# Value products of one attention tile and scores of the next in one run with shared banks; low half of the gated product at the head of a step

## The chip, the core and the metric

The kernel runs on one core of a Trainium2 chip. Its engines work side by side, each through its own instructions in order, and wait for each other by semaphores: TensorE (PE in the rows; PEld is its weight load), VectorE (DVE), ScalarE (ACT), GpSimd (POOL), and SyncE (SP), which here issues all transfers. The metric is the device time of one execution in microseconds, the median of the runs.

## The reference, cut to what matters

```python
# attention in chunks of 64 tokens, 8 heads of 64
scores = scale * np.matmul(q_c, k_c.transpose(0, 1, 2, 4, 3))
attn = np.exp(scores - np.max(scores, axis=-1, keepdims=True))
attn = attn / (np.sum(attn, axis=-1, keepdims=True) + 1e-09)
out = np.matmul(attn, v_c)
# then x of 4608 tokens x 512 through a gated layer of 512 x 1536 x 512,
g = x @ w_gate
silu = g * (1.0 / (1.0 + np.exp(-g)))
val = x @ w_val
y = silu * val @ w_out
# then x / rms * rms_g, and a second gated layer of the same form
```

## The kernel before, in words

The program is written in the order in which each engine runs it: no scheduler moves anything. The first layer works on 9 blocks of 512 tokens, and a block in 12 steps of 128 hidden features (the loop at L1024). Every matrix is held as a high and a low part, so each product is three matmuls of 128x512 (`mm3`, L441).

A step has three groups of 12 matmuls on TensorE: g (`emit_g`), v (`emit_v`) and y (`emit_y`). The y of a step is that of the step before (`prev`). On ScalarE a tanh follows g (L454); on VectorE `product` (L455) makes the gate of it, `v_product` (L471) multiplies by v, ScalarE casts the result to its high part hh (L474), and `lo` (L476) subtracts to give the low part hl. hh and hl feed the y of the next step, where hl is needed by the second matmul (L443). g and v have one PSUM bank each, y has four, and the two banks a0 and a1 are left for attention and for the sums of squares.

Attention comes in 36 tiles of 128 tokens, those of a block during the block before it. From tile 8 on a tile is: `trans_att` (VectorE transposes q and k, L305), `att_s` (32 small matmuls, scores into a0 and a1), `att_m` (VectorE maxima and subtractions L341, L342, ScalarE exp), `att_n` (sums and reciprocal, then GpSimd multiplies), `att_td` in two halves (VectorE transposes p, L376), `att_pv` (32 small matmuls into new tiles in a0 and a1, then two ScalarE copies to xh, L427), and `att_lo` (VectorE, low part xl, L436).

What is done where is set by a table: `put` hangs a function on a position, three positions to a step. Position 0 of a step runs after g, 1 after v and `product`, 2 after y and `v_product` (L1053 to L1069). Before, the tiles of a block start at positions 0, 8, 16 and 24 of its 36. Also in the table: the sums of squares of the block before (`rms_*`; their two matmuls, ssq, use a0), the loads of q, k and v by SP, and, every second step, the loading and conversion (L115 to L121) of a second-layer weight, of which GpSimd, ScalarE and SP make combinations. Step 0 of a block ends the y of the block before, which `evac_y` copies out of PSUM. In block 0 VectorE also converts the weights of the first layer (`conv1`).

The second layer (L1089 on) follows on the same core and has no part in the change.

Of the kernel before, what the change touches and what calls it, by code (L numbers as in the profile page):

```python
# [9 lines left out]
F32 = mybir.dt.float32  # L10
# [9 lines left out]
def tile_kernel(  # L20
# [19 lines left out]
    NT, DM = out.shape  # L40
    DFF = moe_w_gate.shape[1]
    P = 128
    CH = 64
# [267 lines left out]

    prob = {}

    def att_s(i, tags=("a0", "a1")):
        qT, kT = qkT.pop(i)
        sb = [ps.tile([P, 512], F32, tag=tags[z], name=f"s{z}_{i}") for z in range(2)]
        for hp in range(HP):
            for x in range(2):
                for hpar in range(2):
                    c = hpar ^ x  # L320
                    nc.tensor.matmul(
                        sb[x][c * 64:c * 64 + 64, hp * 64:hp * 64 + 64],
                        qT[hp][hpar * 64:hpar * 64 + 64, c * 64:c * 64 + 64],
                        kT[hp][hpar * 64:hpar * 64 + 64, c * 64:c * 64 + 64],
                        start=True,
                        stop=True,
                    )
        score[i] = sb
# [75 lines left out]

    xps = {}

    def att_pv(i, j, tags=("a0", "a1")):
        pT = probT.pop(i)
        xb = [ps.tile([P, 512], F32, tag=tags[c], name=f"xb{c}_{i}") for c in range(2)]
        xb = [t[:, :HP * CH].rearrange("p (h c) -> p h c", h=HP) for t in xb]  # L410
        for hp in range(HP):
            for c in range(2):
                g, n = where[2 * i + c]
                vt = gt[g][2]
                for hpar in range(2):
                    z = (hpar ^ c) * 64
                    nc.tensor.matmul(
                        xb[c][hpar * 64:hpar * 64 + 64, hp, :],
                        vt[z:z + 64, hp, n, :],
                        pT[z:z + 64, hp, c * 64:c * 64 + 64],  # L420
                        start=True,
                        stop=True,
                    )
        xh, xl = x_tiles(0, j)
        o = i * P - blocks[j][0]
        for c in range(2):
            nc.scalar.copy(xh[:, :, o + c * CH:o + (c + 1) * CH], xb[c])  # L427
        xps[i] = xb

    def att_lo(i, j):  # L430
        xb = xps.pop(i)
# [159 lines left out]
    def spread(l, j, pos, n, make):  # L591
# [7 lines left out]
        for z in range(n):  # L599
            put(l, j, pos + z, lambda z=z: step(z))  # L600

    for x, (l, j) in enumerate(seq):
        if x + 1 < len(seq):
            nl, nj = seq[x + 1]
            if nl == 0:
                for n, i in enumerate(tiles_of(nj)):
                    b = 8 * n if x else (0, 11, 19, 26)[n]
                    if i >= 8:
                        put(l, j, b - 1, lambda i=i: trans_att(i))
                    else:  # L610
                        put(l, j, b, lambda i=i: trans_tok(i, ("a0", "a1")))
                    e = 1 if i < 8 else 0
                    put(l, j, b + 1 + e, lambda i=i: att_s(i))
                    put(l, j, b + 2 + e, lambda i=i: att_m(i))
                    put(l, j, b + 3 + e, lambda i=i: att_n(i))
                    if i < 8:
                        put(l, j, b + 6, lambda i=i: att_t(i))
                    else:
                        put(l, j, b + 4, lambda i=i: att_td(i, 0))
                        put(l, j, b + 5, lambda i=i: att_td(i, 1))  # L620
                    e = 0 if i < 8 else 1
                    put(l, j, b + 8 - e, lambda i=i, nj=nj: att_pv(i, nj))
                    put(l, j, b + 9 - e, lambda i=i, nj=nj: att_lo(i, nj))
                    for c in (2 * i, 2 * i + 1):
                        g = where[c][0]
                        if g > 0 and c == groups[g][-1] and g + 2 < len(groups):
                            d = 10 if i < EARLY else 1
                            spread(l, j, b + d, 8, lambda g=g: load_qk(g + 2))
                            spread(l, j, b + d + 8, 3, lambda g=g: load_v(g + 2))
        if x > 0 and seq[x - 1][0] == 0:  # L630
            pj = seq[x - 1][1]
            for d in range(KD):
                put(l, j, 3 + 2 * d, lambda pj=pj, d=d: rms_sq(pj, d))
            put(l, j, 12, lambda pj=pj: rms_split(pj))
            put(l, j, 14, lambda pj=pj: rms_mm(pj))
            for z in range(4):
                put(l, j, 18 + 2 * z, lambda pj=pj, z=z: rms_rec(pj, z))
            put(l, j, 26, lambda pj=pj: rms_newton(pj))
            for d in range(KD):
                put(l, j, 28 + 2 * d, lambda pj=pj, d=d: rms_x(pj, d))  # L640

# [287 lines left out]
    with tc.manual_schedule():  # L929
# [94 lines left out]
        for n, (l, j, f) in enumerate(iters):  # L1024
            def run(p):
                for fn in at.get(3 * n + p, ()):
                    fn()

            head = (l, j) == (0, 0)
            if (j, f) == (1, 0):  # L1030
                conv.close()
                cv = open_pool(conv, "cv2", 2, "right")
            if (j, f) == (NB - 1, 0):
                conv.close()
                attn.close()
                X2 = open_pool(two, "x2", 1, "right")
                x_load(0, 0)
                xops = x_prep(0, 0)
            if (j, f) == (NB - 1, 8):
                x_load(0, 1)  # L1040
                xops = xops + x_prep(0, 1)
            if (j, f) == (NB - 1, 8):
                load_ring(16)

            if head and f == 0:
                issue(later + load_tok(5))
            if head and f in (1, 2):
                issue(load_tok(5 + f))
                if f == 1:
                    issue(load_v(2))  # L1050
            if n + 2 < len(iters) and n + 2 >= NF:
                load_lo(*iters[n + 2])
            sg, product = emit_g(l, j, f)  # L1053
            run(0)
            if prev is not None:
                lo()
            if head:
                conv1(3 * f + 7)
            v_product, lo = emit_v(l, j, f, sg)
            product()  # L1060
            run(1)
            if head:
                conv1(3 * f + 8)
            if prev is not None:
                emit_y(*prev)
                if prev[2] == NF - 1:
                    evac_y(*prev[:2])
            v_product()
            run(2)  # L1069
            if head:  # L1070
                conv1(3 * f + 9)
            if j == NB - 1 and f >= 2:
                for _ in range(3 if f > 6 else 2):
                    if xops:
                        xops.pop(0)()
            prev = (l, j, f)
# [109 lines left out]
```

## Time and profile before

| | us |
|---|---|
| median of three runs | 1839.19 (1836.37 to 1842.35) |
| the profiled execution, its time | 1840.34 |
| its span, first to last instruction | 1838.5 |
| TensorE busy in the span | 1781.2 (97%) |
| VectorE busy | 1275.0 (69%) |
| ScalarE busy | 661.4 (36%) |
| GpSimd busy | 389.9 (21%) |

A busy TensorE is not one at its peak: the end of a matmul is modelled and rows overlap, so a row's length tells little and the distance from one row's start to the next tells how fast it goes. Times in the rows are in us from the start of the span, and a bracket at a row's end gives the idle time of its engine before it and who ended it.

### The profile page before, as it was taken

How to read it: one execution, taken by the hardware profiler on the slowest of the kernel's cores; microseconds unless marked ns; L12 is line 12 of the kernel's file. 1: busy time of each engine (PE TensorE's matmuls, PEld its weight loads, DVE VectorE, ACT ScalarE, POOL GpSimd, SP SyncE). 2: the span in 40 equal slices, each digit the busy share in tenths (PEclk: the TensorE clock that was granted, in tenths of full speed). 3: DMA queues.
4: the chain of work that ended last, by engine and by line, in shares of the span. 5: the costliest groups of instructions: out<-in, count | busy, mean ns of one | idle time of the engine just before them, and what ended most of it. 6: DMA issues, size and time to landing. Idle time of an engine off the chain costs nothing.

```text
span 1838.5 us, 31037 instructions
## 1 busy us (share of the span) xinstructions
PE 1781.2 (97%) x11094; PEld 1518.3 (83%) x11094; DVE 1275.0 (69%) x2358; ACT 661.4 (36%) x1254; POOL 389.9 (21%) x391
## 2 busy tenths in 40 slices
PE   5989999999999999999999999999999999999999
PEld 4767787877878777787888778988898889999999
DVE  7986887877778687886735466845694477468465
ACT  4543322323233233323223333533462344335334
POOL 1001325342343433424022200200020011002000
PEclk7989999999999999999999999999999999999999
DMA  9986667776668676675344476677667767887885
GB/s 250 265 239 159 175 188 212 206 235 163 212 175 232 191 203 214 192 225 160 98 134 164 151 230 193 212 228 215 191 213 229 210 188 235 255 264 262 272 245 182
DMA packets 385034, 379.86 MB, mean 207 GB/s; under 512 B 200048, under 2 KB 235888, under 8 KB 384880
## 3 DMA queue, kind: packets, MB, share of 16 engines
q1 hardware_dynamic: 384880, 377.87, 69.1%
q8 instruction: 89, 1.46, 0.3%
q14 instruction: 65, 0.53, 0.1%
HBM read 316.41 MB, written 61.34 MB: 205 GB/s over the span
## 4 chain that ended last, share of the span: by engine, by line
PE 80%; DVE 10%; DMA 4%; SPq 2%; POOL 2%; ACT 2%; issue 1%; DVEq 0%; ACTq 0%; POOLq 0%
PE y L443 5%; PE ygA L882 4%; PE y L442 4%; PE y L444 4%; PE g L442 4%; PE v L442 4%; PE g L444 4%; PE g L443 4%; PE v L444 4%; PE v L443 4%; PE yvA L882 4%; PE ygC L882 2%; PE yvC L882 2%; DVE pT L376 2%; DVE hl L476 1%
## 5 line engine op out<-in xcount | busy, mean ns | idle before, releaser
L443 PE MATMUL y<-hl,wo 128*128 128x512 f32 x432 | 174.6, 404 | 20.6 <-DVE hl L476 20.4
L442 PE MATMUL y<-hh,wo 128*128 128x512 f32 x432 | 175.2, 406 | 0.0
L442 PE MATMUL g<-xh,wg 128*128 128x512 f32 x432 | 171.7, 397 | 1.2 <-ACT xh L427 0.9
L444 PE MATMUL y<-hh,lo 128*128 128x512 f32 x432 | 171.7, 398 | 0.0
L442 PE MATMUL v<-xh,wv 128*128 128x512 f32 x432 | 170.2, 394 | 1.3 <-DVE sg L471 1.3
L443 PE MATMUL g<-xl,wg 128*128 128x512 f32 x432 | 169.4, 392 | 1.6 <-DVE xl L436 1.6
L444 PE MATMUL g<-xh,lg 128*128 128x512 f32 x432 | 169.3, 392 | 1.0 <-DMA lg<-lo_scratch 1.0
L444 PE MATMUL v<-xh,lv 128*128 128x512 f32 x432 | 168.3, 390 | 0.0
L443 PE MATMUL v<-xl,wv 128*128 128x512 f32 x432 | 168.2, 389 | 0.0
L455 DVE SCALAR_TENSOR_TENSOR sg<-sg,g 128x512 f32<-128x512 f32 x108 | 73.8, 684 | 127.5 <-ACT sg L454 127.4
L454 ACT ACTIVATE sg<-g 128x512 f32<-128x512 f32 x108 | 64.5, 597 | 252.1 <-PE g L444 252.0
L822 POOL TENSOR_TENSOR h<-h,h 128x512 f32<-128x512 f32 (+1 forms) x30 | 37.0, 1234 | 550.9 <-DVE h L800 550.9
L376 DVE STREAM_TRANSPOSE pT<-p 32x128 f32<-32x128 f32 x448 | 135.6, 303 | 11.3 <-POOL p L360 5.2
L474 ACT CAST hh<-sg 128x512 fp32r<-128x512 f32 x108 | 67.1, 622 | 194.2 <-DVE sg L471 193.7
L858 DVE TENSOR_TENSOR hl<-h,hh 128x512 fp32r<-128x512 f32 (+1 forms) x180 | 122.4, 705 | 13.1 <-ACT hh L857 13.0
L443 PEld LDWEIGHTS y<-hl,wo 128*128 128x128 f32 x432 | 83.2, 193 | 45.8 <-DVE hl L476 29.6
L857 ACT CAST hh<-h 128x512 fp32r<-128x512 f32 (+1 forms) x180 | 98.8, 576 | 41.0 <-PE yvA L882 26.1
L783 ACT ACTIVATE sig<-sgt 128x512 f32<-128x512 f32 (+1 forms) x90 | 53.0, 589 | 155.9 <-DVE sgt L791 155.8
L360 POOL TENSOR_TENSOR p<-p,r 128x512 f32<-128x512 f32 x36 | 43.3, 1203 | 286.3 <-DVE r L359 248.8
L784 DVE TENSOR_TENSOR sgt<-sgt,sig 128x512 f32<-128x512 f32 (+1 forms) x90 | 57.7, 641 | 61.7 <-ACT sig L783 61.7
L471 DVE SCALAR_TENSOR_TENSOR sg<-v,sg 128x512 f32<-128x512 f32 x108 | 73.7, 682 | 36.3 <-PE v L444 35.1
L442 PEld LDWEIGHTS y<-hh,wo 128*128 128x128 f32 x432 | 82.9, 192 | 18.9
(769 smaller groups left out, 4619.8 us busy)
## 6 DMA issues: line engine op xcount, KB each, us to landing
wrg<-w_scratch SPq DMA_DIRECT2D x210, 256.0 KB, 3.1
wrv<-w_scratch SPq DMA_DIRECT2D x210, 256.0 KB, 3.1
wro<-w_scratch SPq DMA_DIRECT2D x210, 256.0 KB, 3.0
lg<-lo_scratch SPq DMA_DIRECT2D x96, 256.0 KB, 2.9
lv<-lo_scratch SPq DMA_DIRECT2D x96, 256.0 KB, 3.4
lo<-lo_scratch SPq DMA_DIRECT2D x96, 256.0 KB, 3.8
w_scratch<-wsg SPq DMA_DIRECT2D x42, 256.0 KB, 2.4
w_scratch<-wsv SPq DMA_DIRECT2D x42, 256.0 KB, 2.7
```

Source lines behind the costliest of these rows:

```text
L376: nc.vector.transpose(out=pT[o:o + 32, :, r:r + 32], in_=pt[r:r + 32, :, z, b * 32:b * 32 + 32])
L442: nc.tensor.matmul(o, sh, mh, start=first, stop=False, skip_group_check=free)
L443: nc.tensor.matmul(o, sh, ml, start=False, stop=False, skip_group_check=free)
L444: nc.tensor.matmul(o, sl, mh, start=False, stop=last, skip_group_check=free)
L454: nc.scalar.activation(sg[:, :n], g[:, :n], AF.Tanh, scale=0.5)
L455: return sg, lambda: nc.vector.scalar_tensor_tensor(out=sg[:, :n], in0=sg[:, :n], scalar=1.0, in1=g[:, :n], op0=ALU.add, op1=ALU.mult)
L471: nc.vector.scalar_tensor_tensor(out=sg[:, :n], in0=vv[:, :n], scalar=0.5, in1=sg[:, :n], op0=ALU.mult, op1=ALU.mult)
L474: nc.scalar.copy(hh[:, :n], sg[:, :n])
L784: nc.vector.tensor_mul(t[:, :tw], src[:, :tw], sg[:, :tw])
L857: nc.scalar.copy(hh[:, :tw], src)
L858: nc.vector.tensor_sub(hl[:, :tw], src, hh[:, :tw].bitcast(F32))
L882: mm = lambda l, r, first, last: nc.tensor.matmul(oo, l, r, start=first, stop=last, skip_group_check=True)
```

## The change

`att_both(i)` puts the value products of tile i and the scores of tile i+1 into one run. Both use one pair of tiles in a0 and a1, the products the lower 256 columns, the scores the upper. The copies to xh come behind the whole run (`att_hi`). `score_at` gives the new places: 0, 7, 15 and 23 in block 1, then one every 9 positions; from tile 11 on a run stands behind the v of a step. The transposes of q and k stand one position ahead, the two transposes of p four and three positions ahead, the low part xl one behind. In a step, `lo()` now stands ahead of `emit_g`, and `v_product` ahead of `evac_y`. The rms pieces move by one to three positions, the loads of v two later within a tile.

```diff
--- before.py
+++ after.py
@@ -311,9 +311,10 @@
 
     prob = {}
 
-    def att_s(i, tags=("a0", "a1")):
+    def att_s(i, tags=("a0", "a1"), sb=None):
         qT, kT = qkT.pop(i)
-        sb = [ps.tile([P, 512], F32, tag=tags[z], name=f"s{z}_{i}") for z in range(2)]
+        if sb is None:
+            sb = [ps.tile([P, 512], F32, tag=tags[z], name=f"s{z}_{i}") for z in range(2)]
         for hp in range(HP):
             for x in range(2):
                 for hpar in range(2):
@@ -404,9 +405,10 @@
 
     xps = {}
 
-    def att_pv(i, j, tags=("a0", "a1")):
+    def att_pv(i, j, tags=("a0", "a1"), xb=None, put_off=False):
         pT = probT.pop(i)
-        xb = [ps.tile([P, 512], F32, tag=tags[c], name=f"xb{c}_{i}") for c in range(2)]
+        if xb is None:
+            xb = [ps.tile([P, 512], F32, tag=tags[c], name=f"xb{c}_{i}") for c in range(2)]
         xb = [t[:, :HP * CH].rearrange("p (h c) -> p h c", h=HP) for t in xb]
         for hp in range(HP):
             for c in range(2):
@@ -423,9 +425,28 @@
                     )
         xh, xl = x_tiles(0, j)
         o = i * P - blocks[j][0]
+        xps[i] = xb
+        if put_off:
+            return
+        att_hi(i, j)
+
+    def att_hi(i, j):
+        xb = xps[i]
+        xh, xl = x_tiles(0, j)
+        o = i * P - blocks[j][0]
         for c in range(2):
             nc.scalar.copy(xh[:, :, o + c * CH:o + (c + 1) * CH], xb[c])
-        xps[i] = xb
+
+    NT_ = NT // P
+
+    def att_both(i):
+        both = [ps.tile([P, 512], F32, tag=f"a{z}", name=f"both{z}_{i}") for z in range(2)]
+        if i >= 2 * NW // P:
+            att_pv(i, i * P // NW, xb=both, put_off=True)
+        if i + 1 < NT_:
+            att_s(i + 1, sb=[t[:, HP * CH:] for t in both])
+        if i >= 2 * NW // P:
+            att_hi(i, i * P // NW)
 
     def att_lo(i, j):
         xb = xps.pop(i)
@@ -599,43 +620,52 @@
         for z in range(n):
             put(l, j, pos + z, lambda z=z: step(z))
 
+    def score_at(i):
+        n = i - 8
+        return NP + ((0, 7, 15, 23)[n] if n < 4 else 31 + 9 * (n - 4))
+
     for x, (l, j) in enumerate(seq):
         if x + 1 < len(seq):
             nl, nj = seq[x + 1]
             if nl == 0:
                 for n, i in enumerate(tiles_of(nj)):
-                    b = 8 * n if x else (0, 11, 19, 26)[n]
                     if i >= 8:
-                        put(l, j, b - 1, lambda i=i: trans_att(i))
+                        a = score_at(i)
+                        e = score_at(i + 1)
+                        b = a - 1 - x * NP
+                        if i == 8:
+                            put(0, 0, a, lambda: att_both(7))
+                        put(0, 0, a - 1, lambda i=i: trans_att(i))
+                        put(0, 0, a + 1, lambda i=i: att_m(i))
+                        put(0, 0, a + 2, lambda i=i: att_n(i))
+                        put(0, 0, e - 4, lambda i=i: att_td(i, 0))
+                        put(0, 0, e - 3, lambda i=i: att_td(i, 1))
+                        put(0, 0, e, lambda i=i: att_both(i))
+                        put(0, 0, e + 1, lambda i=i, nj=nj: att_lo(i, nj))
                     else:
+                        b = (0, 11, 19, 26)[n]
                         put(l, j, b, lambda i=i: trans_tok(i, ("a0", "a1")))
-                    e = 1 if i < 8 else 0
-                    put(l, j, b + 1 + e, lambda i=i: att_s(i))
-                    put(l, j, b + 2 + e, lambda i=i: att_m(i))
-                    put(l, j, b + 3 + e, lambda i=i: att_n(i))
-                    if i < 8:
+                        put(l, j, b + 2, lambda i=i: att_s(i))
+                        put(l, j, b + 3, lambda i=i: att_m(i))
+                        put(l, j, b + 4, lambda i=i: att_n(i))
                         put(l, j, b + 6, lambda i=i: att_t(i))
-                    else:
-                        put(l, j, b + 4, lambda i=i: att_td(i, 0))
-                        put(l, j, b + 5, lambda i=i: att_td(i, 1))
-                    e = 0 if i < 8 else 1
-                    put(l, j, b + 8 - e, lambda i=i, nj=nj: att_pv(i, nj))
-                    put(l, j, b + 9 - e, lambda i=i, nj=nj: att_lo(i, nj))
+                        put(l, j, b + 8, lambda i=i, nj=nj: att_pv(i, nj))
+                        put(l, j, b + 9, lambda i=i, nj=nj: att_lo(i, nj))
                     for c in (2 * i, 2 * i + 1):
                         g = where[c][0]
                         if g > 0 and c == groups[g][-1] and g + 2 < len(groups):
                             d = 10 if i < EARLY else 1
                             spread(l, j, b + d, 8, lambda g=g: load_qk(g + 2))
-                            spread(l, j, b + d + 8, 3, lambda g=g: load_v(g + 2))
+                            spread(l, j, b + d + (8 if i < 8 else 10), 3, lambda g=g: load_v(g + 2))
         if x > 0 and seq[x - 1][0] == 0:
             pj = seq[x - 1][1]
             for d in range(KD):
                 put(l, j, 3 + 2 * d, lambda pj=pj, d=d: rms_sq(pj, d))
-            put(l, j, 12, lambda pj=pj: rms_split(pj))
-            put(l, j, 14, lambda pj=pj: rms_mm(pj))
+            put(l, j, 14, lambda pj=pj: rms_split(pj))
+            put(l, j, 17, lambda pj=pj: rms_mm(pj))
             for z in range(4):
-                put(l, j, 18 + 2 * z, lambda pj=pj, z=z: rms_rec(pj, z))
-            put(l, j, 26, lambda pj=pj: rms_newton(pj))
+                put(l, j, 19 + 2 * z, lambda pj=pj, z=z: rms_rec(pj, z))
+            put(l, j, 27, lambda pj=pj: rms_newton(pj))
             for d in range(KD):
                 put(l, j, 28 + 2 * d, lambda pj=pj, d=d: rms_x(pj, d))
 
@@ -1050,10 +1080,10 @@
                     issue(load_v(2))
             if n + 2 < len(iters) and n + 2 >= NF:
                 load_lo(*iters[n + 2])
+            if prev is not None:
+                lo()
             sg, product = emit_g(l, j, f)
             run(0)
-            if prev is not None:
-                lo()
             if head:
                 conv1(3 * f + 7)
             v_product, lo = emit_v(l, j, f, sg)
@@ -1063,9 +1093,9 @@
                 conv1(3 * f + 8)
             if prev is not None:
                 emit_y(*prev)
-                if prev[2] == NF - 1:
-                    evac_y(*prev[:2])
             v_product()
+            if prev is not None and prev[2] == NF - 1:
+                evac_y(*prev[:2])
             run(2)
             if head:
                 conv1(3 * f + 9)
```

VectorE, steps 1 and 2 of block 5, before (in the names the numbers are block, step and a buffer; sg_5_1 from v is the product of v, hl_5_1 the low part, pT the transposed p, cmg and crg a weight in conversion):

```order
L476 TENSOR_TENSOR hl_5_0_6677<-sg_5_0_6654,hh_5_0_6676 128x512
L455 SCALAR_TENSOR_TENSOR sg_5_1_6765<-sg_5_1_6765,g_5_1_6752 128x512
L376 STREAM_TRANSPOSE pT_6803<-p_6730 32x4x32 x8
L471 SCALAR_TENSOR_TENSOR sg_5_1_6765<-v_5_1_6787,sg_5_1_6765 128x512
L376 STREAM_TRANSPOSE pT_6803<-p_6730 32x4x32 x8
L115 TENSOR_SCALAR cmg_1_6863<-w64g_1_6660 128x512
L118 SCALAR_TENSOR_TENSOR cmg_1_6863<-w64g_1_6660,cmg_1_6863 128x512
L121 SCALAR_TENSOR_TENSOR crg_1_6824<-crg_1_6824,cmg_1_6863 128x512
L476 TENSOR_TENSOR hl_5_1_6801<-sg_5_1_6765,hh_5_1_6800 128x512
L455 SCALAR_TENSOR_TENSOR sg_5_2_6886<-sg_5_2_6886,g_5_2_6873 128x512
```

The same place now, from the copies of y at the end of step 0 on:

```order
L530 COPY ysb_0_4_6745<-y_4_3_5660 128x512
L497 TENSOR_TENSOR hl_5_0_6710<-sg_5_0_6675,hh_5_0_6709 128x512
L305 STREAM_TRANSPOSE qT_6782<-xq_5932 128x512
L305 STREAM_TRANSPOSE kT_6784<-xk_5933 128x512
L476 SCALAR_TENSOR_TENSOR sg_5_1_6780<-sg_5_1_6780,g_5_1_6767 128x512
L492 SCALAR_TENSOR_TENSOR sg_5_1_6780<-v_5_1_6796,sg_5_1_6780 128x512
L457 TENSOR_TENSOR xl_6_6831<-both_24_6812,xh_6_6830 128x4x64
...
L342 TENSOR_REDUCE m_6884<-both_24_6812 128x4
...
L115 TENSOR_SCALAR cmg_1_6898<-w64g_1_6694 128x512
L118 SCALAR_TENSOR_TENSOR cmg_1_6898<-w64g_1_6694,cmg_1_6898 128x512
L121 SCALAR_TENSOR_TENSOR crg_1_6858<-crg_1_6858,cmg_1_6898 128x512
L497 TENSOR_TENSOR hl_5_1_6810<-sg_5_1_6780,hh_5_1_6809 128x512
```

The transposes of p have gone from in front of hl_5_1; low part xl, maxima and subtractions of the next tile and the conversion stand there now, and the transposes of q and k (qT, kT) stand behind hl_5_0 in the step in which the run needs them.

TensorE, the end of v in step 2 of block 5, before, with its waits:

```order
L444 MATMUL v_5_2_6895<-xh_5_5718,lv_5_2_6637 128x512
L417 MATMUL xb_24_6911<-pT_6803,xv_5774 64x64 [waits PE_49]
...
L417 MATMUL xb_24_6912<-pT_6803,xv_5774 64x64 [waits DVE_49,PE_49]
...
L417 MATMUL xb_24_6912<-pT_6803,xv_5774 64x64 x2
L442 MATMUL y_5_0_6826<-hh_5_1_6800,wo_0_512 128x512 [waits Activation_49]
L443 MATMUL y_5_0_6826<-hl_5_1_6801,wo_0_512 128x512 [waits DVE_49]
```

The end of v in step 1 of block 5, now:

```order
L465 MATMUL v_5_1_6796<-xh_5_5627,lv_5_1_6580 128x512
L419 MATMUL both_24_6812<-pT_6677,xv_5677 64x64 [waits PE_49]
...
L419 MATMUL both_24_6813<-pT_6677,xv_5677 64x64 [waits PE_49]
...
L419 MATMUL both_24_6813<-pT_6677,xv_5677 64x64 x2
L322 MATMUL both_24_6812<-kT_6784,qT_6782 64x64 [waits DVE_49]
...
L322 MATMUL both_24_6813<-kT_6784,qT_6782 64x64 x2
L463 MATMUL y_5_0_6860<-hh_5_0_6709,wo_0_421 128x512 [waits Activation_49]
L464 MATMUL y_5_0_6860<-hl_5_0_6710,wo_0_421 128x512
```

The scores (from kT, qT) stand directly behind the products (from pT, xv) in the same two tiles; the wait for VectorE is at the first score matmul, and y of hl_5_0 behind it has none of its own.

VectorE, from the operation behind ssq on, block 5, before (ms, rr are the rms pieces):

```order
L545 TENSOR_SCALAR ms_7154<-ssq_7151 128x512
L305 STREAM_TRANSPOSE qT_7205<-xq_6069 128x512
...
L476 TENSOR_TENSOR hl_5_4_7121<-sg_5_4_7085,hh_5_4_7120 128x512
L455 SCALAR_TENSOR_TENSOR sg_5_5_7183<-sg_5_5_7183,g_5_5_7170 128x512
L436 TENSOR_TENSOR xl_6_6930<-xb_25_7185,xh_6_6929 128x4x64
...
L471 SCALAR_TENSOR_TENSOR sg_5_5_7183<-v_5_5_7218,sg_5_5_7183 128x512
```

and now:

```order
L566 TENSOR_SCALAR ms_7272<-ssq_7269 128x512
L115 TENSOR_SCALAR cmv_1_7280<-w64v_1_7079 128x512
...
L497 TENSOR_TENSOR hl_5_5_7235<-sg_5_5_7202,hh_5_5_7234 128x512
L377 STREAM_TRANSPOSE pT_7306<-p_7162 32x4x32 x8
L476 SCALAR_TENSOR_TENSOR sg_5_6_7304<-sg_5_6_7304,g_5_6_7291 128x512
L377 STREAM_TRANSPOSE pT_7306<-p_7162 32x4x32 x8
L577 RECIPROCAL rr_7274<-rr_7274 128x128
L492 SCALAR_TENSOR_TENSOR sg_5_6_7304<-v_5_6_7321,sg_5_6_7304 128x512
L497 TENSOR_TENSOR hl_5_6_7335<-sg_5_6_7304,hh_5_6_7334 128x512
L305 STREAM_TRANSPOSE qT_7390<-xq_6543 128x512
L305 STREAM_TRANSPOSE kT_7392<-xk_6544 128x512
```

ms has moved from the end of step 4 to the end of step 5, and both transposes of p and a reciprocal now follow it ahead of the product of v of step 6.

## Rows read from the trace of the kernel before

**Rows 1.** Busy time by stage: block 0, then blocks 1 to 7.

```profile
core 0: us, PE busy (x) PEld busy (x) DVE busy (x) ACT busy (x) POOL busy (x), PEclk, DMA share, GB/s
36.00:166.00 130.00, 115.93 (x725) 91.69 (x726) 113.05 (x204) 62.08 (x111) 4.70 (x4) 0.94 0.83 237
166.00:931.00 765.00, 748.50 (x4832) 600.34 (x4831) 586.96 (x1218) 230.90 (x456) 265.80 (x289) 0.99 0.66 192
```

**Rows 2.** Waits of TensorE, blocks 1 to 7: us, times, longest.

```profile
PE y L443 <- DVE hl L476: 16.4, 18, 2.3
```

**Rows 3.** TensorE timeline (start, length, operation): g of steps 1.0, 5.1, 5.11, 6.0, 8.0.

```profile
165.84 0.39 PE L442 MATMUL g<-xh,wg 128*128 128x512 f32 x1
...
615.75 0.39 PE L442 MATMUL g<-xh,wg 128*128 128x512 f32 x1
...
707.96 0.39 PE L442 MATMUL g<-xh,wg 128*128 128x512 f32 x1
...
716.12 0.39 PE L442 MATMUL g<-xh,wg 128*128 128x512 f32 x1
...
930.97 0.39 PE L442 MATMUL g<-xh,wg 128*128 128x512 f32 x1
```

**Rows 4.** TensorE timeline, block 5: value products, the wait behind them; a score run's end.

```profile
629.76 0.39 PE L444 MATMUL v<-xh,lv 128*128 128x512 f32 x1
630.08 0.69 PE L417 MATMUL xb<-pT,xv 64*64 64x64 f32 x32
630.70 0.51 PE L442 MATMUL y<-hh,wo 128*128 128x512 f32 x1
633.49 0.51 PE L443 MATMUL y<-hl,wo 128*128 128x512 f32 x1 [2.28 <-DVE hl L476]
...
639.56 0.50 PE L442 MATMUL v<-xh,wv 128*128 128x512 f32 x1
639.90 0.39 PE L443 MATMUL v<-xl,wv 128*128 128x512 f32 x1
```

**Rows 5.** TensorE timeline, block 5: the two ssq matmuls, the next g.

```profile
653.82 0.39 PE L542 MATMUL ssq<-ah,ones 128*128 128x512 f32 x1
...
654.29 0.40 PE L442 MATMUL g<-xh,wg 128*128 128x512 f32 x1
```

**Rows 6.** TensorE, block 3: the wait in step 2, and the stretch behind it.

```profile
410.99 0.80 PE L443 MATMUL y<-hl,wo 128*128 128x512 f32 x1 [2.30 <-DVE hl L476]
...
412.00:417.00 5.00, 5.00 (x13) 3.92 (x12) 2.68 (x6) 0.62 (x1) 1.19 (x1) 0.50 0.49 174
```

**Rows 7.** VectorE timeline, block 5.

```profile
606.05 0.39 DVE L115 TENSOR_SCALAR cmo<-w64o 128x512 uint32<-128x512 uint32 x1
...
607.87 0.69 DVE L476 TENSOR_TENSOR hl<-sg,hh 128x512 fp32r<-128x512 f32 x1
...
615.95 0.69 DVE L509 COPY ysb<-y 128x512 f32<-128x512 f32 x1 [0.67 <-PE y L444]
...
617.16 0.41 DVE L341 TENSOR_REDUCE m<-s 128x4 f32<-128x256 f32 x1
...
626.05 2.52 DVE L376 STREAM_TRANSPOSE pT<-p 32x128 f32<-32x128 f32 x8
628.61 0.57 DVE L115 TENSOR_SCALAR cmg<-w64g 128x512 uint32<-128x512 uint32 x1
...
631.69 1.75 DVE L476 TENSOR_TENSOR hl<-sg,hh 128x512 fp32r<-128x512 f32 x1
...
633.96 0.70 DVE L305 STREAM_TRANSPOSE qT<-xq 128x512 f32<-128x512 f32 x1
...
666.25 0.94 DVE L556 RECIPROCAL rr<-rr 128x128 f32<-128x128 f32 x1
```

**Rows 8.** ScalarE timeline, block 5.

```profile
609.72 0.60 ACT L454 ACTIVATE sg<-g 128x512 f32<-128x512 f32 x1 [4.15 <-PE g L444]
...
630.81 0.65 ACT L427 CAST xh<-xb 128x256 fp32r<-128x256 f32 x2 [1.48 <-PE xb L417]
```

## The prediction

> **What bounds the kernel now.** Read first the busy time by stage, to see where TensorE is the limit and where VectorE is: in the first block VectorE is busy 113.05 of 130.00 us, in blocks 1 to 7 TensorE has 748.50 of 765.00 us and VectorE 586.96 [rows 1]. The blocks 1 to 7, where the attention tiles are woven in, are the stage that the change rewrites. Then the waits of TensorE in that stage: one only, the second matmul of a y group waits for hl (VectorE, L476), 18 times, 16.4 us in all [rows 2]. Third, the timeline of TensorE, for what its busy time hides. A step without attention takes 716.12 - 707.96 = 8.16 us for 36 matmuls, 0.227 us each, and the seven blocks take 930.97 - 165.84 = 765.1 us for 84 steps, which alone would be 685.4 us [rows 3]. So 79.7 us of the stage are something else, far more than the waits:
>
> A run of 32 small matmuls takes 0.62 us up to the next large one (630.08 to 630.70). Around it something is lost twice: the run starts 0.32 us after the last large matmul, 0.09 more than 0.227, and the second large one comes 0.34 us after the first (639.56 to 639.90), 0.11 more [rows 4]. That is 0.82 us a run; there are 56 (scores and value products of tiles 8 to 35), 45.9 us. The two ssq matmuls take 654.29 - 653.82 = 0.47 us a block, 3.3 us [rows 5]. What is left, 79.7 - 45.9 - 3.3 = 30.5 us, is the 16.4 us of hl waits and what follows them: about 0.3 us to start again, and in part a slower clock. After the wait of 2.30 us that ends at 410.99 the granted clock is 0.50 from 412 to 417 (the 1.2 GHz level), so some 2.5 us go there, while after a wait of 2.28 us in another block the matmuls keep 0.39 us [rows 4, 6]. About 2 of the 30.5 I count as small leftovers that stay.
>
> **The change, part by part.**
>
> One run in place of two: value products of tile i and scores of tile i+1 stand together. 28 + 28 runs become 27 double ones (tiles 8 to 34) and two single ones (scores of 8, products of 35). The matmuls are the same, 2 x 0.62 = 1.24 us a double run, and one of two changes goes, 0.09 + 0.11 = 0.20 us. No row shows what the seam inside a double run costs; it lies between nothing and the 0.20 us of a full change, so the gain lies between 27 x 0.20 = 5.4 us and none. I take 5.4, since at the seam operand shapes and types stay as they are within a run. The Trainium skill (TensorEngine Tiling (Array Packing), Key Properties) says that TensorE drains when the tiling mode changes, not when the tile does; by that the seam is free, and a rule by which each group drained would give a time 5.4 us longer.
>
> The low half hl at the head of a step: hl of step n now stands on VectorE ahead of what step n+1 hands over after its g, so ahead of the transposes of p or of q and k. It doesn't become ready earlier by itself: its input is the cast hh on ScalarE, behind the product of v. New in front of it are the pieces that now fall in the last third of a step: low half of x, maxima and subtractions, and the weight conversion. So its two worst places have to be counted. Durations are of [rows 7, 8], on VectorE 0.60 us from start to start for a 128x512 operation.
>
> Place A, steps 1 and 2 of a block, where the six long waits stand. T is the start of g of step 1, 615.75 in block 5 [rows 3]. Before, hl of step 1 ends at 633.44, T + 17.7, and TensorE would have taken it at 630.70 + 0.34 = 631.04, T + 15.3: the 2.3 us [rows 4, 7]. Two transposes of p of 2.52 us and a conversion that ran beside GpSimd (628.61 to 631.69, 3.08 us) stood ahead of it. Now: the last y copy T + 0.2 to 0.8, hl of step 0 to 1.4, transposes of q and k (1.3) to 2.7, product of g, behind g's own 2.72 us and the tanh of 0.60, about 3.6 to 4.2, product of v, behind v's end, about T + 5.6 to 6.2. The double run starts at T + 5.5 and ends at 6.8; the two ScalarE copies xh start 0.1 later (630.81 after 630.70) and take 0.65, to 7.6; low half of x, two 128x256 operations at 0.41, to 8.4; maxima and subtractions, four of 0.41, to 10.1; conversion 1.8 us (606.05 to 607.87) or 3.1 beside GpSimd, to 11.9 or 13.2; hl 0.6 or 1.75, to T + 12.5 or 14.9. It is wanted in step 2's y, at T + 8.16 + 1.44 + 5.44 + 0.23 = 15.3. Margin 0.4 to 2.8 us: the long waits go. The Trainium skill (PSUM — Partial Sum Buffer, PSUM bank collisions raise a hardware error) says that two engines must not touch one bank in the same partitions at once; that speaks against shared banks, for it makes xh wait for the scores too, and the count above already puts the copies behind the whole run. Without that rule they would be 0.6 us earlier and the margin that much wider.
>
> Place B, steps 5 to 7, with ssq and the reciprocals moved. U is the start of g of step 6. The row of ssq reads from U - 0.47 on, its VectorE operation runs about U + 0.2 to 0.8, conversion to 2.6, hl of step 5 to 3.2 (wanted at U + 5.8), first transposes of p (2.55) to 5.8, product 6.4, second transposes 8.9, reciprocal (0.94) 9.8, product of v 10.4. The v bank is wanted by v of step 7 at U + 0.1 + 8.16 + 2.72 = 11.0: margin 0.6, or 0.7 short if GpSimd runs beside the conversion, at most 7 x 0.7 = 5 us. Then hh (0.6), hl of step 6 to 11.7, transposes of q and k to 13.0; the double run's second half wants them at U + 8.3 + 5.5 + 0.6 = 14.4. hl of step 7 then ends some 3.6 us into step 8 and is wanted at 5.7.
>
> So 28.5 us of waits and their train go; for B and the closer spacing of block 1 (7 to 8 positions a tile where later ones have 9) I leave 2 us, between 0 and 7.
>
> Moved besides, at no cost. The y copies go behind the product of v: they are wanted one y group, over 5.4 us, later, and the product no longer stands behind the copy at 615.95, which waited for y [rows 7]. ssq goes one step later and newton by a third of a step, with no matmul of this stage waiting for them. The DMAs: the load of v stands one position behind the products that free its buffer, was two; SP can wait some 5 us there with the next step's low-half weights behind it, which are issued two steps (16 us) ahead of use. Block 0: hl passes only a few operations, and VectorE sets the time there (113.05 of 130 us [rows 1]); what TensorE no longer waits for hl it waits for the next VectorE result. I take 0, between a gain of 5 us and no change.
>
> Sum against the profiled execution: 1840.34 - 5.4 - 28.5 + 2 = 1808.4. The median of the runs shown is 1.15 us under it: 1807.3, taken as 1807.
>
> **The rivals.**
>
> Waits come back at another place. hl now stands behind four kinds of work in steps 1 and 7, with a margin of 0.4 at its worst. For it: VectorE is 77% busy, in order, and its operations grow beside GpSimd (hl from 0.69 to 1.75 us). Against it: the work of a tile is spread over 9 positions, was 8 with a hole of 12. Of the 18 waits six are long, 1.6 to 2.3 us, one in each of blocks 1 to 6; if they stay and only the twelve short ones (0.2 to 0.3 us, 0.6 with the restart) and the 27 changes go: 1839.2 - 5.4 - 7 = 1827.
>
> The transposes of q and k become the wait (the slower side). They now stand behind hl on VectorE, which stands behind hh on ScalarE, in the same step in which the double run wants them, in mid-run. If they came late by 1.5 us, with 0.3 to start again, 27 x 1.8 = 48.6 us: 1807 + 49 = 1856. It decides from 32/27 = 1.2 us a run on, a wait of 0.9: the second half would start at T + 5.5 + 0.6, so the transposes would end at T + 7.0. Against it: T + 2.7 in A and 14.4 - 13.0 = 1.4 us of margin in B. If the clock fell too, as at 412 to 417 [rows 6], it would cost more still.
>
> It does little: GpSimd contention and the reciprocals eat the gain, so that the stage keeps its 30 us of waits in other rows and only the changes go, or not even these: 1834 to 1839.
>
> **How the numbers follow.** My forecast, 1800 to 1816, 0.72; waits that come back, 1816 to 1833, 0.16; little, 0.06; slower, 0.06. The low end is 1807 without the 2 us of leftover waits and with the 5 us of block 0: 1800. The high end takes in a seam that costs 0.20 (5.4 us), the worst of B (5) and, of the waits that come back, some six tenths, to 1826; above it stay 0.06 of these, 0.06 and 0.06, together 0.18. About 0.3% (5.5 us) is what a measurement of this kernel can tell from no change: faster 0.72 + 0.16 = 0.88, same 0.06, slower 0.06.
>
> **What would show it.** Right: 27 runs of 64 small matmuls of about 1.24 us with 0.09 and 0.11 around them; the wait of y for hl nearly gone from the waits of TensorE; seven blocks in about 765.1 - 32 = 733 us; no stretch at clock 0.50 after block 0. Wrong: a seam that takes 0.2 us; hl waits in step 2 or 8 of a block; TensorE waiting for L305, or for the product of v at the start of v of step 7; block 0 longer than its 130 us.

## The result, and the profile after

The changed kernel takes 1805.08 us (median of 4 runs, 1804.60 to 1805.25), the kernel before 1837.79 beside it: a ratio of 0.9819 with an interval of 0.9807 to 0.9831. 1807 was predicted, 1800 to 1826 as the range. The profiled execution of after took 1805.25 us with a span of 1803.4, that of before 1840.34 with 1838.5.

The busy time by stage, to be set beside [rows 1]: the window on core 0, then busy time and count of TensorE, its weight loads, VectorE, ScalarE and GpSimd, the granted clock, the DMA share and GB/s.

```profile
36.00:165.30 129.30, 115.64 (x725) 91.12 (x725) 112.49 (x203) 61.76 (x111) 4.19 (x4) 0.94 0.84 239
165.30:896.00 730.70, 729.24 (x4831) 596.94 (x4830) 576.28 (x1218) 228.67 (x456) 260.00 (x289) 1.00 0.69 201
```

Blocks 1 to 7 take 34.2 us less by their first g (below), and their clock is now 1.00 as a mean and in every stretch of 5 us. Block 0 is what it was. The first g of block 1 and of block 8, as in [rows 3]:

```profile
165.28 0.39 PE L463 MATMUL g<-xh,wg 128*128 128x512 f32 x1
...
896.19 0.39 PE L463 MATMUL g<-xh,wg 128*128 128x512 f32 x1
```

That is 730.9 us for the seven blocks, 765.1 before. Such stage times are those of one profiled execution for each kernel; in the experiment below that edits block 0 alone it takes 730.0 us, so that a difference of 1 us in it tells little. All waits of TensorE that the profile lists between them (line and tile, what was waited for, us, times, longest), which stand against the 16.4 us of [rows 2]:

```profile
PE both L322 <- DVE kT L305: 1.2, 4, 0.4
```

The wait for hl is gone from this stage. A new one is there: the scores, in the middle of a double run, wait for the transposes of q and k. First a double run without it (block 5), then one with it:

```profile
649.55 0.39 PE L465 MATMUL v<-xh,lv 128*128 128x512 f32 x1
649.87 0.69 PE L419 MATMUL both<-pT,xv 64*64 64x64 f32 x32
650.38 0.65 PE L322 MATMUL both<-kT,qT 64*64 64x64 f32 x32
650.96 0.50 PE L463 MATMUL y<-hh,wo 128*128 128x512 f32 x1
651.30 0.39 PE L464 MATMUL y<-hl,wo 128*128 128x512 f32 x1
...
675.67 0.69 PE L419 MATMUL both<-pT,xv 64*64 64x64 f32 x32
676.63 0.69 PE L322 MATMUL both<-kT,qT 64*64 64x64 f32 x32 [0.27 <-DVE kT L305]
677.25 0.50 PE L463 MATMUL y<-hh,wo 128*128 128x512 f32 x1
```

And the run in step 10 of block 3:

```profile
466.41 0.69 PE L419 MATMUL both<-pT,xv 64*64 64x64 f32 x32
467.14 1.02 PE L322 MATMUL both<-kT,qT 64*64 64x64 f32 x32
468.09 0.50 PE L463 MATMUL y<-hh,wo 128*128 128x512 f32 x1
```

From the first small matmul to the next large one it is 650.96 - 649.87 = 1.09 us, where two runs of 0.62 [rows 4] had been counted. Before it stand 0.32 us and behind it 0.34, as around a single run in [rows 4]. So 64 small matmuls cost one surround and not two, and also 0.15 us less in themselves. In the second run the two starts lie 0.96 us apart in place of 0.51, and the run takes 1.58 us. The listed waits are in step 10 of blocks 2, 4, 5 and 6. In block 3 none is listed, but the two starts lie 0.73 us apart and the run takes 468.09 - 466.41 = 1.68 us: time is lost inside the scores too. The five runs take 1.57 to 1.74 us where the other 22 take 1.09 to 1.10, so they lose 2.7 us together, more than the 1.2 us listed.

### The profile page after: what moved, and what is told of

Its sections match the earlier page's. It is cut to its first block, busy times and chain, and to the rows that moved or that the text cites. A ratio compares the mean times of both kernels' runs of the same rounds, so it can differ in the third digit from the quotient of the medians.

```text
span 1803.4 us, 31009 instructions
## 1 busy us (share of the span) xinstructions
PE 1763.7 (98%) x11094; PEld 1516.2 (84%) x11094; DVE 1267.7 (70%) x2358; ACT 659.4 (37%) x1254; POOL 384.0 (21%) x391
## 4 chain that ended last, share of the span: by engine, by line
PE 80%; DVE 10%; DMA 3%; issue 2%; ACT 2%; SPq 2%; POOL 1%; DVEq 0%; ACTq 0%; POOLq 0%
PE ygA L912 5%; PE y L463 4%; PE y L465 4%; PE y L464 4%; PE g L465 4%; PE g L463 4%; PE g L464 4%; PE v L463 4%; PE v L464 4%; PE v L465 4%; PE yvA L912 4%; PE ygC L912 2%; PE yvC L912 2%; PE ygD L912 1%; SPq L294 1%
## 5 line engine op out<-in xcount | busy, mean ns | idle before, releaser
L464 PE MATMUL y<-hl,wo 128*128 128x512 f32 x432 | 169.1, 391 | 1.4 <-DVE hl L497 1.4
L888 DVE TENSOR_TENSOR hl<-h,hh 128x512 fp32r<-128x512 f32 (+1 forms) x180 | 122.2, 704 | 13.9 <-ACT hh L887 13.8
L361 POOL TENSOR_TENSOR p<-p,r 128x512 f32<-128x512 f32 x36 | 37.9, 1054 | 369.6 <-DVE r L360 368.1
L463 PEld LDWEIGHTS g<-xh,wg 128*128 128x128 f32 x432 | 81.7, 189 | 22.4 <-DVE sg L476 4.4
L463 PEld LDWEIGHTS v<-xh,wv 128*128 128x128 f32 x432 | 81.1, 188 | 20.5 <-DVE sg L492 3.7
```

Of the source, the lines that this page charges most:

```text
L463: nc.tensor.matmul(o, sh, mh, start=first, stop=False, skip_group_check=free)
L464: nc.tensor.matmul(o, sh, ml, start=False, stop=False, skip_group_check=free)
L888: nc.vector.tensor_sub(hl[:, :tw], src, hh[:, :tw].bitcast(F32))
```

## The experiments

The question: most of the 34.2 us that the changed stage gained were forecast to come from waits. Did the waits go because hl now stands at the head of a step (**theory H**), or because the pieces of a tile have new places and a wider spacing (**theory S**)? And is the merged run worth the 0.20 us a tile of the saved surround, or more? Ratios are to the kernel before, run beside each.

**Only the low half at the head, in the kernel before.**

```
+            if prev is not None:
+                lo()
             sg, product = emit_g(l, j, f)
             run(0)
-            if prev is not None:
-                lo()
```

> The kernel before with one edit: the low half hl moved to the head of a step, attention as before. Theory S (the new places and the wider spacing of the attention pieces removed the long waits): in the kernel before, nothing that VectorE does after the g of step 2 stands ahead of hl of step 1, so the six long waits of 1.6 to 2.3 us stay; only the twelve short ones (0.6 us each with the restart) go: 1838 - 7 = 1831 us. Theory H (the place of hl in the step removed them): all 28 us go, 1810 us.

1832.76 us, ratio 0.9973 (0.9957 to 0.9990); blocks 1 to 7 take 757.6 us, 7.5 less than before. The twelve short waits of [rows 2] are gone, the six long ones are not. The list of waits of these blocks, and three of the six (blocks 1, 3 and 6):

```profile
PE y L443 <- DVE hl L476: 13.0, 6, 2.5
```

```profile
191.67 0.50 PE L443 MATMUL y<-hl,wo 128*128 128x512 f32 x1 [1.48 <-DVE hl L476]
...
407.71 0.80 PE L443 MATMUL y<-hl,wo 128*128 128x512 f32 x1 [2.49 <-DVE hl L476]
...
735.43 0.79 PE L443 MATMUL y<-hl,wo 128*128 128x512 f32 x1 [2.48 <-DVE hl L476]
```

All six stand in step 2 of a block, as before. There the transposes of p and the conversion beside GpSimd still run ahead of hl, and moving hl past other work doesn't help. The clock still falls behind some of them (0.72 from 736 to 741). Theory H fails for the long waits. It holds for the short ones: 16.4 - 13.0 = 3.4 us of waits and twelve restarts of 0.3 are 7.0 of the 7.5 us. By the medians, with the kernel before run beside it (1839.46 us), the gain is 6.7 us.

**Only the places: tiles of a block from positions 3, 11, 18 and 26, in the kernel before.**

```
-                    b = 8 * n if x else (0, 11, 19, 26)[n]
+                    b = (3, 11, 18, 26)[n] if x else (0, 11, 19, 26)[n]
```

> The kernel before with one edit: from block 1 on its four tiles start at positions 3, 11, 18 and 26 of the block, not at 0, 8, 16 and 24, so that the two transposes of p (2.5 us each) of the first tile stand behind hl of step 1 and not ahead of it. Runs stay single, hl stays behind what follows g. Theory S: the six long waits go with what hangs on them, some 20 us; short ones may come elsewhere: 1812 to 1822 us. Theory H (only hl at the head removes them): 1835 to 1840 us.

1822.08 us, ratio 0.9913 (0.9895 to 0.9930); blocks 1 to 7 take 746.9 us, 18.3 less. Their waits:

```profile
PE y L443 <- DVE hl L476: 4.4, 6, 0.8
PE s L321 <- DVE xl L436: 1.4, 4, 0.8
```

The six long waits are gone, with no moved hl and no merged run: theory S, though the time stands at the upper end of what it forecast. Of short ones there are now one a block in step 10, in blocks 1 to 6, where a transpose of p and a normalising product stand ahead of hl on VectorE, and four of the scores. About 2.7 us come back behind block 7: from there to the end it is 910.3 us, 907.5 before. One wait of TensorE for ScalarE in the last stage is 2.40 us long (1.40 before), and behind it the granted clock is 0.66 from 1670 to 1675, where before it doesn't fall; together these make up the 2.7 us. The profiled execution is also the slowest of its four (1825.41 us).

These places are not those of the change, which come every 9 positions from tile 11 on and with which the rms pieces move; those places are in the next run.

**The change without the low half at the head.**

```
-            if prev is not None:
-                lo()
             sg, product = emit_g(l, j, f)
             run(0)
+            if prev is not None:
+                lo()
```

> The changed kernel with hl put back behind what follows g; runs, places and the order of the y copies as changed. Theory S: hl has a margin of 1 us or more in most steps; a few short waits in steps 6 and 9, where two transposes of p of 2.5 us now stand ahead of it, and the five waits for the transposes of k in step 10 go: 1805 to 1810 us. Theory H: the waits of y for hl come back, 1825 to 1833 us.

1806.91 us, ratio 0.9830 (0.9811 to 0.9849), 1.8 more than the changed kernel by the medians, which were not run beside each other; blocks 1 to 7 take 732.3, 1.4 more. Five waits for hl come back, two in block 1 and one each in blocks 2, 4 and 6, none of them long ones of step 2, and the waits for the transposes go:

```profile
PE y L464 <- DVE hl L497: 3.3, 5, 1.3
```

So in the new places the head is worth 1 to 2 us, close to what can be told. That is about its 3.3 us of waits with five restarts, less the 3 us that the waits for the transposes cost (below). All of it lies in block 1, where the tiles come every 7 or 8 positions: the block takes 106.8 us without the head and 104.6 with it, while blocks 2 to 7 take 0.8 us less without it.

**The change with two runs in place of one.** The products go behind the g of a step, the scores stay behind v; banks and places are otherwise those of the change.

```
+    held = {}
+
+    def att_first(i):
+        both = [ps.tile([P, 512], F32, tag=f"a{z}", name=f"both{z}_{i}") for z in range(2)]
+        held[i] = both
+        if i >= 2 * NW // P:
+            att_pv(i, i * P // NW, xb=both, put_off=True)
...
+                        put(0, 0, e - 1, lambda i=i: att_first(i))
                         put(0, 0, e, lambda i=i: att_both(i))
```

> The changed kernel with the double run taken apart: the value products of a tile one third of a step earlier (after g), the scores where they are (after v), the same shared banks, the copies where they are. If a run costs a fixed 0.17 us beside 0.46 us for 32 matmuls (0.63 for 32, 1.09 for 64 in the trace), and 0.20 us in the large matmuls around it, then 27 x 0.37 = 10 us more: 1815 us. If the two halves cost the same apart, with no fixed part, only 27 x 0.20 = 5.4: 1810.5 us. If merging gave nothing: 1805 us.

1814.04 us, ratio 0.9866 (0.9846 to 0.9887), 9.0 more than the changed kernel; blocks 1 to 7 take 737.5, 6.6 more (the rest lies outside the stage that the edit touches). A tile's two runs in block 5:

```profile
652.44 0.39 PE L471 MATMUL g<-xh,lg 128*128 128x512 f32 x1
652.76 0.69 PE L419 MATMUL both<-pT,xv 64*64 64x64 f32 x32
653.39 0.50 PE L469 MATMUL v<-xh,wv 128*128 128x512 f32 x1
653.73 0.39 PE L470 MATMUL v<-xl,wv 128*128 128x512 f32 x1
...
656.02 0.39 PE L471 MATMUL v<-xh,lv 128*128 128x512 f32 x1
656.34 0.69 PE L322 MATMUL both<-kT,qT 64*64 64x64 f32 x32
656.96 0.50 PE L469 MATMUL y<-hh,wo 128*128 128x512 f32 x1
657.30 0.39 PE L470 MATMUL y<-hl,wo 128*128 128x512 f32 x1
```

653.39 - 652.76 = 0.63 and 656.96 - 656.34 = 0.62 us, with 0.32 ahead and 0.34 behind each, as in [rows 4]. A second run costs 0.62 + 0.63 - 1.09 = 0.16 us of its own and 0.20 of surround: 27 x 0.36 = 9.7 us. In the stage 6.6 are seen, since with two runs only one wait for the transposes is left (0.2 us), and those cost the merged kernel about 3.

This kernel also shows the places and the head together without the merging: 765.1 - 737.5 = 27.6 us of the stage. The change's places without the head are worth about 765.1 - 732.3 - 9.7 = 23.1 us, more than the 18.3 of the places 3, 11, 18 and 26, with which ten short waits remain. How much of that is the spacing and how much the moved rms pieces was not run.

**The scores of a tile written twice, one behind the other, in the changed kernel.** Work is added: a double run becomes one of 96.

```
+            qk = qkT[i + 1]
+            if i >= 2 * NW // P:
+                att_s(i + 1, sb=[t[:, HP * CH:] for t in both])
+                qkT[i + 1] = qk
             att_s(i + 1, sb=[t[:, HP * CH:] for t in both])
```

> The changed kernel with the 32 score matmuls of a tile written twice in the 27 double runs (work added, same values): runs of 96. Fixed part and 0.46 us for each further 32: 27 x 0.46 = 12.4 us more, 1817.5 us, runs of 1.55 us. If instead every group of 32 costs 0.63 when its kind repeats and the pair of products and scores is what overlaps: 27 x 0.63 = 17 us more, 1822 us.

1816.52 us, ratio 0.9880 (0.9862 to 0.9899), 11.4 more than the change; blocks 1 to 7 take 742.9 us, 11.9 more. One such run:

```profile
285.62 0.39 PE L469 MATMUL v<-xh,lv 128*128 128x512 f32 x1
285.94 0.69 PE L419 MATMUL both<-pT,xv 64*64 64x64 f32 x32
286.45 1.11 PE L322 MATMUL both<-kT,qT 64*64 64x64 f32 x64
287.50 0.50 PE L467 MATMUL y<-hh,wo 128*128 128x512 f32 x1
287.83 0.39 PE L468 MATMUL y<-hl,wo 128*128 128x512 f32 x1
```

1.56 us for 96, beside 1.09 for 64 and 0.63 for 32: 0.47 us for each 32 and 0.16 fixed, whatever the length, with the same 0.32 and 0.33 around. That settles the size of a change between large and small matmuls: 0.36 us. The Trainium skill says (TensorEngine Tiling (Array Packing), Key Properties) that a change of the tiling mode drains TensorE and a change of the tile does not. The runs agree in kind: the seam between products and scores costs nothing, each way in and out does. The section gives no price.

**The second normalising product of a block one third of a step later, in the changed kernel.**

```
-                put(l, j, 28 + 2 * d, lambda pj=pj, d=d: rms_x(pj, d))
+                put(l, j, (28, 31, 32, 34)[d], lambda pj=pj, d=d: rms_x(pj, d))
```

> The changed kernel with one VectorE operation of 0.66 us (second product of the normalisation of a block) moved from ahead of the transposes of q and k in step 10 to behind them. If it is what makes the double run of step 10 wait in blocks 2 to 6 (0.25 to 0.42 us and the restart, 0.5 us each): 5 x 0.5 = 2.5 us less, 1802.5 us, and no wait for L305. If the transposes are late for another reason (hl of step 9 ahead of them): 1805 us.

1801.98 us, ratio 0.9809 (0.9794 to 0.9825); blocks 1 to 7 take 727.7, 3.2 less than the change, with no wait of TensorE listed. VectorE in step 10 of block 5 of the changed kernel first (the run's second half wanted kT at 676.18, 0.51 behind its start):

```profile
674.02 0.68 DVE L497 TENSOR_TENSOR hl<-sg,hh 128x512 fp32r<-128x512 f32 x1
674.62 0.74 DVE L594 SCALAR_TENSOR_TENSOR ysb<-ysb,rg,rr 128x512 f32<-128x512 f32 x1
675.28 0.70 DVE L305 STREAM_TRANSPOSE qT<-xq 128x512 f32<-128x512 f32 x1
675.91 0.66 DVE L305 STREAM_TRANSPOSE kT<-xk 128x512 f32<-128x512 f32 x1
```

Then with the product later, and the run that follows:

```profile
673.20 0.68 DVE L497 TENSOR_TENSOR hl<-sg,hh 128x512 fp32r<-128x512 f32 x1
673.80 0.70 DVE L305 STREAM_TRANSPOSE qT<-xq 128x512 f32<-128x512 f32 x1
674.43 0.67 DVE L305 STREAM_TRANSPOSE kT<-xk 128x512 f32<-128x512 f32 x1
...
675.59 0.73 DVE L594 SCALAR_TENSOR_TENSOR ysb<-ysb,rg,rr 128x512 f32<-128x512 f32 x1
```

```profile
674.83 0.69 PE L419 MATMUL both<-pT,xv 64*64 64x64 f32 x32
675.34 0.65 PE L322 MATMUL both<-kT,qT 64*64 64x64 f32 x32
```

One operation of 0.66 us, for which TensorE does not wait, stood ahead of the transposes. Behind them it costs nothing that shows. This version is 3.1 us under the changed kernel by the medians, which were not run beside each other; the 3.2 us of the stage, all of them in blocks 2 to 6, and the vanished wait say the same, and so does the next kernel, which was run beside this one and differs from the change only in an order that costs nothing in the stage: 1806.31 us. This version is the fastest of all.

**The copies of y ahead of the product of v again, in the changed kernel.**

```
                 emit_y(*prev)
+                if prev[2] == NF - 1:
+                    evac_y(*prev[:2])
             v_product()
-            if prev is not None and prev[2] == NF - 1:
-                evac_y(*prev[:2])
```

> The changed kernel with the copies of y back ahead of the product of v at a block's end. The product of v of step 0 then stands behind two copies that end 0.9 us into step 1, so hl of step 0 comes some 1.5 us later, and with it the transposes of q and k in step 1, which had some 2.5 us of margin: 1805 to 1807 us. If that order was a part of the gain: 6 or 7 blocks x 1 us, 1811 us.

1806.31 us, ratio 0.9833 (0.9818 to 0.9849); blocks 1 to 7 take 731.0, as in the change (730.9). The order of these copies is worth nothing that can be measured here; the 1.2 us by which the medians differ lie, in the profiled executions, outside the stage.

**Part of the low-half subtractions of block 0 moved from VectorE to GpSimd, in the changed kernel.** It was to test whether VectorE sets the time of block 0: 20 of the 36 subtractions of 0.6 us go.

```
-        nc.vector.tensor_sub(lo, r, hi.bitcast(F32))
+        (nc.gpsimd if f >= 2 and nm != "o" else nc.vector).tensor_sub(lo, r, hi.bitcast(F32))
```

> The changed kernel with 20 of the 36 subtractions that make the low parts of the first layer's weights moved from VectorE to GpSimd, which is nearly idle in block 0 (4.2 us of 129). Each is 0.6 us on VectorE. If VectorE sets the time of block 0, as the prediction took it in order to give the earlier hl there no gain: up to 12 us less, 1793 to 1800 us. If it doesn't: 1805 us. If GpSimd and VectorE hinder each other: above 1805 us.

1810.44 us, ratio 0.9853 (0.9837 to 0.9869), 5.4 slower than the change. The loss is in block 0 alone: 135.3 us from its first g to that of block 1, where the change takes 129.7; blocks 1 to 7 take 730.0.

```profile
36.08:171.35 135.27, 117.05 (x725) 91.35 (x725) 117.94 (x184) 61.85 (x111) 33.12 (x24) 0.93 0.81 228
```

In this window VectorE has 19 operations fewer than in the change and is busy 5.5 us longer. One operation on GpSimd, and one on VectorE that runs beside it:

```profile
69.12 1.36 POOL L139 TENSOR_TENSOR lv<-crv,wv 128x512 fp32r<-128x512 f32 x1 [2.54 <-ACT wv L131]
```

```profile
69.36 1.67 DVE L118 SCALAR_TENSOR_TENSOR cmo<-w64o,cmo 128x512 uint32<-128x512 uint32 x1
```

The second takes 0.69 us where GpSimd is idle, as at the same place of the changed kernel:

```profile
67.98 0.69 DVE L118 SCALAR_TENSOR_TENSOR cmo<-w64o,cmo 128x512 uint32<-128x512 uint32 x1
```

So each move saved 0.6 us and lengthened what ran beside it by about 0.9 us. VectorE was not relieved, so what the block takes with less work on VectorE stays open. But the block grew by 5.6 us as VectorE's busy time grew by 5.5, and of the waits of TensorE that are listed in it all but one of 0.9 us for ScalarE are for VectorE, none for GpSimd: that agrees with a stage whose time VectorE sets.

## Why the prediction was right, point by point

**The stage and its excess.** The forecast for blocks 1 to 7 was 685.4 + 79.7 - 5.4 - 28.5 + 2 = 733.2 us; it is 730.9. The sum for the profiled execution was 1808.4 against 1805.25: of the 3.15 us, 2.3 are here and the rest is spread before block 0, in it and behind block 7, in parts under half a us.

**The waits, 28.5 us less 2 left over: right.** With two runs a tile, places and head together took 27.6 us out of the stage, against the 26.5 of the sum. That the clock comes back with the waits was right too: 1.00 in the whole stage, and no stretch at half speed. What follows the waits, which the prediction took as a remainder, can be read from the trace of before: each wait costs 0.28 us more than its idle time (18 times, 5.0 us), and the granted clock is below 1 behind three of the six long ones, 0.69, 0.54, 0.78, 0.80 and 0.86 in the 5 us from 190, 410, 415, 520 and 525. Counting the missing share of each, that is an estimate of 6.7 us, and 16.4 + 5.0 + 6.7 = 28.1 us. Of the five waits of 2.28 to 2.30 us two have such a stretch behind them and three have none, so this part is not fixed; the 13 executions of the kernel before beside which the head was tried go from 1834.48 us (mean granted clock 0.991) to 1842.94 (0.986). The split was left open by the prediction, and the runs make it: the places 3, 11, 18 and 26 alone take 18.3 us, the change's own places some 23, the head alone 7.5, and with the new places in, the head is worth 1 to 2. The count of place A rests on what stands ahead of hl, not on where hl was written, and that was the right half to count.

**Place A, right, at its late end.** In block 5 T is 591.83. VectorE there, in the changed kernel:

```profile
598.96 0.76 DVE L457 TENSOR_TENSOR xl<-both,xh 128x256 fp32r<-128x256 f32 x2 [0.80 <-ACT xh L438]
...
601.21 1.10 DVE L115 TENSOR_SCALAR cmg<-w64g 128x512 uint32<-128x512 uint32 x1
602.35 1.66 DVE L118 SCALAR_TENSOR_TENSOR cmg<-w64g,cmg 128x512 uint32<-128x512 uint32 x1
...
605.08 0.68 DVE L497 TENSOR_TENSOR hl<-sg,hh 128x512 fp32r<-128x512 f32 x1
```

hl ends at 605.76, T + 13.9, between the 12.5 and 14.9 counted. The steps to it were off by up to 1.1 us in both directions: the conversion took 605.08 - 601.21 = 3.9 us, 0.8 more than the 3.1 of its late case, and hl itself 0.68 and not 1.75. The second y matmul that uses it starts at 606.97, unheld.

**Place B, short by 0.2 us, inside its leftover.** U is 635.74. hl of step 5 ran beside GpSimd (1.22 us), the product of v of step 6 came at U + 10.5 to 11.1 where 10.4 was counted as its end, and v of step 7 started a quarter of a us late:

```profile
646.22 0.63 DVE L492 SCALAR_TENSOR_TENSOR sg<-v,sg 128x512 f32<-128x512 f32 x1
```

```profile
646.43 0.39 PE L465 MATMUL g<-xh,lg 128*128 128x512 f32 x1
646.90 0.50 PE L463 MATMUL v<-xh,wv 128*128 128x512 f32 x1
647.23 0.40 PE L464 MATMUL v<-xl,wv 128*128 128x512 f32 x1
```

The two starts lie 0.47 us apart where 0.227 is usual, and the next one 0.33. In the five blocks 2 to 6 this is some 1.6 us in all, too short for the profile to list as a wait. The margin of 0.6 was lost mainly to what hl took beside GpSimd; the prediction had allowed for GpSimd beside the conversion (its 0.7-short case). The 2 us left over hold it.

**The merged run, right in kind, mis-sized.** The seam is free, as taken. But 2 x 0.62 = 1.24 us a double run was too much, since each run has 0.16 us of fixed cost of its own besides the 0.20 around it; the row 630.08 to 630.70 of [rows 4] can't tell the fixed part from the part for each matmul, and the prediction put all of it on the matmuls. The term of 5.4 us is 9.7 (27 x 0.36).

**The rival of the transposes: small, but real, and not where it was looked for.** Places A and B were counted, and the transposes were in time in both: in B kT ends at 649.44, U + 13.7, where 13.0 was counted; the scores start at U + 14.6. They were late in step 10, where the normalising product stands between hl and them. The count has no place C for that, though it names the pieces that VectorE gets in the last third of a step. It cost some 3 us and not 48.6, being five runs of 27 that lose 0.5 to 0.65 us each (2.7 us; the moved product gave 3.2). Two of the prediction's own signs of being wrong thus came true, at small size: TensorE waits for L305, and v of step 7 starts late. So two misses, 4.3 us too little gain from the runs and 3.2 us of waits not foreseen, nearly cancel, and the waits gave 1.1 us more than the sum had: that the stage is only 2.3 us off is in part luck.

**Block 0 and the moved pieces at no cost: right.** Block 0 takes 129.7 us (129.9 before), so the 0 taken holds; that VectorE sets its time agrees with the kernel with the subtractions on GpSimd, but no run relieved VectorE there. The order of the y copies gives nothing. The loads of v hold nobody up: no wait for them stands in the list of the stage.

## What to carry to other kernels

When an engine waits for a result of another, count what stands ahead of that result on its producer in every step of a block in which different work falls in between, not only in the two that look worst: here a third place held 3 us. Moving the long work out of the way took away the long waits; moving the result itself to an earlier place in the program took away only short ones. Two bursts of small matmuls put side by side save the surround of one and a fixed part inside it; runs of one, two and three lengths tell these parts from the cost of a matmul. Work that nobody waits for, as the normalising product here, belongs behind the operand of a run and not ahead of it, which was one number in a table.

## What was unexpected of the hardware

A run of 64x64 matmuls in float32, written in turn to the four quarters of the array, takes 0.16 us plus 0.47 us for each 32 matmuls, in lengths of 32, 64 and 96 (0.63, 1.09, 1.56 us), and 0.20 us more in its large neighbours (0.09 ahead and 0.11 behind).

A VectorE operation with its data in SBUF can grow by more beside GpSimd than the move of work to GpSimd saves: from 0.69 to 1.67 us in block 0 where the move saved 0.6, and a conversion of three operations to 3.9 us in place A, where 1.8 is its time alone [rows 7]. The Trainium skill says (SBUF — State Buffer, Who interferes with whom) that VectorE and GpSimd share a read and a write port to SBUF and that an operation of VectorE with two inputs there contends with one of GpSimd that reads it; L118, with two inputs, agrees with that; L115, with one, grew too (1.10 us in place A, 0.39 in [rows 7]), which that statement doesn't cover. Each of the moves of a 0.6 us subtraction cost some 0.28 us net (5.6 us for 20).
